# Attention outputs kept as features by tokens: row sums spread by transfers, the projection's operand in DRAM, VectorE and SyncE in source order

## The chip, the cores and the metric

The kernel runs on one core of one Trainium2 chip. The metric is the device time of one execution in microseconds (us). "Before" is the kernel as it was, "after" the kernel with the change below.

## The reference

The reference is one transformer block with adaptive layer norm, for 2048 tokens of 576 features, all in float32. The attention has 32 heads of 18 features; the gated feed-forward part has 4608 hidden features.

```
mod = (silu(c) @ w_mod).reshape(1, 6, 1, 576)      # sa, ca, ga, sb, cb, gb
h = layernorm(x) * (1 + ca) + sa
q, k, v = split(h @ wqkv)                          # 32 heads of 18
p = softmax(q @ k.T * 18 ** -0.5)                  # 2048 x 2048 for each head
x = x + ga * ((p @ v) @ wo)
h = layernorm(x) * (1 + cb) + sb
x = x + gb * ((sigmoid(h @ w_gate) * (h @ w_up)) @ w_down)
```

## The kernel before

Matrix products are taken in the fast float32 form, whose operands are rounded. To keep precision each operand is split into a rounded high part and a low part (the rest), and a product is the sum of three: high by high, high by low, low by high. A "copy to float32r" makes the high part, a subtraction the low part.

**Attention.** A unit is one pair of heads for one half (1024) of the queries; there are 32 units, first the 16 pairs for half 0, then for half 1. A unit has 16 steps (`kt`), one for each 128 keys. A step computes four transposed score tiles ("t", line 927: keys by queries, with the row maximum carried as two extra features of q), their exponentials on ScalarE (line 931), and four value products ("v", line 548), which collect in one PSUM bank. The values matrix has a column of ones, so that the sum of the exponentials comes out as feature 18 of each head. Beside that, a step does four of the 64 score tiles ("m", line 446) whose row maxima (line 452 on VectorE) the next unit needs. In most units two neighbouring maxima tiles are joined: ScalarE writes relu of the differences (line 455), and VectorE reduces once (line 457); that moves 8 of 64 operations a unit from VectorE to ScalarE. Units in `SINGLE` don't do that. PSUM tiles of "m", "t" and everything else are drawn by `bank()` from a ring of seven.

The order within a step is a string, one for even and one for odd `kt`. "k" stands for taking the finished sums out of PSUM (`taken`), "w" for work beside attention. There is one "w" in each two steps, so a unit is eight pairs of steps with one "w" each. At a "w" the kernel does, in this order, the outputs of the unit before (at `kt` 3), the spreading of the next unit's maxima (`spread`, line 485, four small transfers of `mrows` into the rows of q), and one piece of the generator `rows0` or `rows1`.

`load_heads(u + 2)` stands at the top of unit u. It issues eight transfers on SyncE's queue: for each head of the pair the high and low parts of q (36 and 18 rows of 4 KB) and of k (36 and 18 rows of 10 KB).

**Outputs.** `outputs()` transposes the finished 128x512 tile (32 rows for each head and query chunk, features by queries) in four TensorE transposes to tokens by features (line 572), takes the reciprocal of the sums on VectorE (line 576), copies the tile on ScalarE (line 587) and multiplies on GpSimd into `Oa` or `big` (line 591).

**Projection.** `project_o(t)` handles one tile of 128 tokens in pieces: transpose the outputs to features by tokens and split them (piece 1), the same for the last 64 features in the first half (piece 2), then two half-width products with `wo` of 14 matmuls each in the first half and 9 in the second (line 685, pieces 3 and 4). `rows0` does this for half 0, then the second layer norm and the operands of the gated stage; `rows1` projects half 1 as far as feature 384, and `last_rows` adds the remaining features during the gated stage, from `oend` in DRAM.

**Beside that** GpSimd splits w_down for the later stage in units 4 to 15 (`down_parts`, lines 841 to 848), with loads paced by the steps of attention.

**Order.** TensorE follows the source order in attention (a manual schedule). The order on the other engines and on SyncE's queue is written by a planner, which goes by its own estimate of times. Each engine, and each queue of transfers, works strictly in the order that it was given.

**Gated stage.** 18 blocks of 256 hidden features for each half of the tokens, with seven products for each block of a fast 2x2 scheme (line 1028) and the down projection (line 1064).

The lines of the strings:

```
for does in (("vtmmttmvtm", "tmttkwmtmm") if plain else ("vmmttmmtvt", "mtkttmwmmt"))[kt % 2]:
    ...
    elif does == "w":
        if kt == 3:
            outputs()
```

Of the kernel before, what the change touches and what calls it, by code (L numbers as in the profile page):

```python
# [15 lines left out]
F32 = mybir.dt.float32  # L16
# [24 lines left out]
FROM0, FROM1 = 15 * 16, 27 * 16 + 5  # L41
# [7 lines left out]
SINGLE = (0, 1, 16, 17, 18, 19, 20, 27, 28, 29)  # L49
# [6 lines left out]
def tile_block(ctx, tc, x_in, wqkv, wo, w_gate, w_up, w_down, c_in, w_mod, out):  # L56
# [24 lines left out]
    turns = {"s": 0, "to": 64 + 4 * LEAD, "bank": 0}  # L81
# [155 lines left out]
    oend = dram.tile([P, 8, D - DL], F32, name="oend")  # L237
# [288 lines left out]
    Os = [Oa]  # L526
# [10 lines left out]
    pending = []  # L537

# [18 lines left out]
    def taken():  # L557

        if "whole" in state:
            half, p, acc = state.pop("whole")  # L560
            oT = epool.tile([P, 512], F32, name="oT")
            nc.scalar.copy(oT, acc)
            state["end"] = (half, p, oT)

    def outputs():

        if "end" not in state:
            return
        half, p, oT = state.pop("end")
        tp = bank().rearrange("p (b q) -> p b q", q=P)  # L570
        for b in range(4):
            nc.tensor.transpose(tp[:, b, :], oT[:, b * P : (b + 1) * P], ident)  # L572

        tq = tp.rearrange("p b (j e) -> p j b e", e=32)
        rec = epool.tile([P, 4, 4], F32, name="rec")
        nc.vector.reciprocal(rec, tq[:, :, :, DH])
        if half == 1 and p == H // 2 - 1:
            state["last"] = epool.tile([P, 512], F32, name="oT")[:, 0 : 16 * DH].rearrange("p (t e) -> p t e", t=8)
            for h in range(2):
                nc.vector.tensor_tensor(  # L580
                    state["last"][:, :, h * DH : (h + 1) * DH].rearrange("p (c b) e -> p c b e", c=2),
                    tq[:, 2 * h : 2 * h + 2, :, 0:DH],
                    rec[:, 2 * h : 2 * h + 2, :].unsqueeze(3).to_broadcast([P, 2, 4, DH]),
                    op=ALU.mult,
                )
            return
        nc.scalar.copy(oT, tp.rearrange("p b q -> p (b q)"))
        tq = oT.rearrange("p (b j e) -> p j b e", j=4, e=32)
        for h in range(2):
            f0 = (2 * p + h) * DH  # L590
            nc.gpsimd.tensor_tensor(
                Os[half][:, :, f0 : f0 + DH].rearrange("p (c b) e -> p c b e", c=2),
                tq[:, 2 * h : 2 * h + 2, :, 0:DH],
                rec[:, 2 * h : 2 * h + 2, :].unsqueeze(3).to_broadcast([P, 2, 4, DH]),
                op=ALU.mult,
            )
# [6 lines left out]
    def load_wo():  # L603
# [31 lines left out]
        for _ in range(4):  # L635
            yield

    def project_o(t):

        wo_h, wo_l, we = weights  # L640
        T, T_ = temp([P, 2048], F32R), temp([P, 2048], F32)
        xt, full, od = T_[:, 0:D], T_[:, 1024:1536], T_[:, 1536:1664]
        if t >= 8:
            xt = raws.tile([P, 2, 3, 256], F32, name="raw1", bufs=2).rearrange("p v t c -> p (v t c)")[:, 0:D]
        nc.gpsimd.dma_start(xt, x_rows[:, t, :])
        src = Os[t // 8][:, t % 8, :]
        n = 4 if t < 8 else DL // P
        oh = T[:, 0 : n * P]
        ol = T[:, 512 : 512 + n * P]
        pt = bank()  # L650
        for i in range(n):
            nc.tensor.transpose(pt[:, i * P : (i + 1) * P], src[:, i * P : (i + 1) * P], ident)
        if t >= 12:
            nc.vector.tensor_copy(oh, pt[:, 0 : n * P])
            nc.vector.tensor_sub(ol, pt[:, 0 : n * P], oh.bitcast(F32))
        else:
            full = full[:, 0 : n * P]
            nc.vector.tensor_copy(full, pt[:, 0 : n * P])
            nc.gpsimd.tensor_copy(oh, full)
            nc.gpsimd.tensor_sub(ol, full, oh.bitcast(F32))  # L660
        yield
        if t < 8:
            om = T[:, 1024:1152]
            omh = T[:, 1152:1280]
            nc.gpsimd.tensor_copy(
                od.rearrange("p (a e) -> p a e", e=64), src[:, DM:D].unsqueeze(1).to_broadcast([P, 2, 64])
            )
            pt = bank()
            nc.tensor.transpose(pt[:, 0:P], od, ident)
            nc.vector.tensor_copy(od, pt[:, 0:P])  # L670
            nc.gpsimd.tensor_copy(om[0:64], od[0:64])
            nc.gpsimd.tensor_copy(omh[64:P], od[64:P])
            nc.gpsimd.tensor_sub(om[64:P], od[64:P], omh[64:P].bitcast(F32))
            yield
        for h in range(2):
            cols = slice(h * HALF, (h + 1) * HALF)
            ts_ = []
            for i in range(n):
                a, b = oh[:, i * P : (i + 1) * P], ol[:, i * P : (i + 1) * P]
                ts_ += [(a, wo_h[:, i, cols]), (a, wo_l[:, i, cols]), (b, wo_h[:, i, cols])]  # L680
            if t < 8:
                ts_ += [(om, we[:, 0, cols]), (om, we[:, 1, cols])]
# [6 lines left out]
        if t >= 8:  # L689
            nc.gpsimd.dma_start(x1p[:, t - 8, :], xt)  # L690
# [589 lines left out]
```

## Time and profile before

| | |
|---|---|
| median of 3 runs | 2932.13 us (2930.23 to 2935.79) |
| profiled execution | 2929.86 us, span 2927.5 us, granted clock 0.995 |
| attention, first to last score step | about 236 to 1594 us |
| gated stage | about 1599 us to the end |
| bytes moved | 429 MB, mean 147 GB/s |

Times in the profile count from the start of the span; the execution adds 2.4 us around it. "Busy" is the time in which an engine had an instruction running. An idle time is put down to the engine or transfer that released it. DMA share is the mean busy share of the core's 16 DMA engines.

### The profile page before, as it was taken

Reading aid. Unit: us, or ns where it says so; the run is one execution under the profiler, and the core shown is the slowest. Engines: PE = TensorE matmul, PEld = TensorE weight load, DVE = VectorE, ACT = ScalarE, POOL = GpSimd, SP = SyncE. Lnnn points to the kernel's source line nnn. Section 1 sums busy time; section 2 is a strip of 40 time slices with the busy share of each in tenths; the row PEclk is TensorE's granted clock in tenths of the full one; section 3 lists DMA queues with packets and bytes.
Section 4 is the critical chain, followed back from the end, with each engine's and each line's share of the span. In section 5 each row is a group of like instructions: output and inputs, shape, how many; then the busy total and the mean of one; then the engine's idle time right before and its main releaser. Section 6 shows DMA issues by size and latency. Waiting matters only on the chain.

```text
span 2927.5 us, 46356 instructions
## 1 busy us (share of the span) xinstructions
PE 2848.3 (97%) x17141; PEld 1879.6 (64%) x17141; DVE 2218.6 (76%) x4023; ACT 1581.4 (54%) x2955; POOL 649.4 (22%) x829
## 2 busy tenths in 40 slices
PE   7999999999999999999999899999999999999998
PEld 6964333333444444444443788877888888888888
DVE  7277888888899988999982878789777555555555
ACT  3216889999987778998788333333332111111111
POOL 3122014544213110761102222233221100000000
PEclk9999999999999999999999999999999999999999
DMA  5344124333212110222125866677556844554443
GB/s 180 120 157 128 52 76 140 133 120 123 84 56 76 35 56 23 101 98 66 52 87 177 284 216 234 231 277 247 207 201 233 301 170 167 167 168 167 159 159 136
DMA packets 136745, 429.25 MB, mean 147 GB/s; under 512 B 18884, under 2 KB 56520, under 8 KB 124232
## 3 DMA queue, kind: packets, MB, share of 16 engines
q1 hardware_dynamic: 120472, 344.99, 35.0%
q0 software_dynamic: 16048, 81.31, 7.9%
q8 instruction: 135, 2.21, 0.3%
q14 instruction: 90, 0.74, 0.1%
HBM read 267.77 MB, written 157.95 MB: 145 GB/s over the span
## 4 chain that ended last, share of the span: by engine, by line
PE 82%; DVE 7%; ACT 4%; DMA 3%; issue 3%; SPq 1%; POOL 0%; POOLq 0%; ACTq 0%; DVEq 0%
PE o L548 16%; PE d L1064 14%; PE x L1028 12%; PE s L446 11%; PE s L927 10%; PE bu L1028 4%; PE bg L1028 4%; PE s L274 4%; ACT p L931 3%; PE s L325 2%; PE s L685 2%; DVE mx L452 1%; DVE w L1020 1%; DMA B<-hs 1%; PE s L572 1%
## 5 line engine op out<-in xcount | busy, mean ns | idle before, releaser
L452 DVE TENSOR_REDUCE mx<-s 128x1 f32<-128x512 f32 x1696 | 1076.6, 684 | 126.3 <-PE s L446 108.3
L931 ACT ACTIVATE p<-s 128x512 f32<-128x512 f32 x2048 | 1068.4, 610 | 146.7 <-PE s L446 75.2
L446 PE MATMUL s<-k,q 54*128 54x512 f32 x1920 | 608.4, 451 | 12.2 <-ACT p L931 6.6
L548 PE MATMUL o<-p,vaug 128*32 128x512 f32 x4096 | 554.8, 607 | 0.5 <-ACT p L931 0.4
L927 PE MATMUL s<-q,k 56*128 56x512 f32 x1920 | 552.6, 425 | 1.3 <-DMA q<-mrows 0.8
L1064 PE MATMUL d<-wd,hh 128*128 128x288 f32 x2304 | 468.3, 297 | 20.8 <-DVE Oa L1068 20.2
L927 PEld LDWEIGHTS s<-q,k 56*128 56x128 f32 x1920 | 260.5, 186 | 295.2 <-DVE mx L452 184.7
L446 PEld LDWEIGHTS s<-k,q 54*128 54x128 f32 x1920 | 273.6, 184 | 250.3 <-ACT p L931 172.3
L1064 PEld LDWEIGHTS d<-wd,hh 128*128 128x128 f32 x2304 | 373.4, 188 | 35.6 <-DVE Oa L1068 26.4
L1068 DVE TENSOR_TENSOR Oa<-Oa,d 128x288 f32<-128x288 f32 x576 | 256.0, 452 | 125.5 <-PE d L1064 120.3
L1064 PE MATMUL d<-wd,hl 128*128 128x288 f32 x1152 | 340.7, 296 | 0.0
L1028 PE MATMUL x<-k,w 128*128 128x512 f32 x1008 | 242.4, 390 | 4.7 <-DVE u L1239 2.4
L1040 ACT ACTIVATE u<-u 128x512 f32<-128x512 f32 x72 | 45.5, 632 | 318.3 <-DVE u L1228 312.1
L1064 PEld LDWEIGHTS d<-wd,hl 128*128 128x128 f32 x1152 | 216.9, 188 | 0.0
L1028 PEld LDWEIGHTS x<-k,w 128*128 128x128 f32 x1008 | 186.7, 188 | 42.5 <-DVE u L1239 3.5
L548 PEld LDWEIGHTS o<-p,vaug 128*32 128x32 f32 x4096 | 83.4, 108 | 163.9 <-issue 151.4
L1037 ACT ACTIVATE sg<-x 128x512 f32<-128x512 f32 x36 | 21.5, 599 | 304.3 <-PE x L1028 304.3
L1070 POOL DMA_DIRECT2D out_dram<-Oa x16 | 8.7, 543 | 606.0 <-DVE Oa L1068 606.0
L455 ACT ACTIVATE over<-s 128x512 f32<-128x512 f32 x176 | 105.1, 597 | 33.5 <-PE s L446 28.4
L1028 PE MATMUL x<-big,w 128*128 128x512 f32 x504 | 120.6, 390 | 1.0 <-issue 1.0
L1028 PE MATMUL x<-w,w 128*128 128x512 f32 x504 | 121.0, 390 | 0.0
L457 DVE CUSTOM_DVE_ANT_0 over<-s,over 128x512 f32<-128x512 f32 x176 | 120.2, 683 | 0.3
(232 smaller groups left out, 3605.1 us busy)
## 6 DMA issues: line engine op xcount, KB each, us to landing
ws<-w SPq DMA_DIRECT2D x126, 640.0 KB
w<-ws SPq DMA_DIRECT2D x126, 640.0 KB
wd<-wds SPq DMA_DIRECT2D x36, 1152.0 KB
k<-kd SPq DMA_DIRECT2D x60, 360.0 KB
wds<-w POOLq DMA_DIRECT2D x18, 1152.0 KB, 4.5
k<-kd SPq DMA_DIRECT2D x60, 180.0 KB
w<-in_B_w_down_dram POOLq DMA_DIRECT2D x18, 576.0 KB, 4.3
q<-qd SPq DMA_DIRECT2D x64, 144.0 KB
```

The source lines that it names most:

```text
L274: nc.tensor.matmul(acc, w, hT[:, t, cols], start=n == 0, stop=n == len(ts_) - 1)
L325: nc.tensor.matmul(acc[:, 0:HALF], hT[:, k, rows], w, start=n == 0, stop=n == len(ts_) - 1,)
L446: nc.tensor.matmul(sp, qs[rows, qt * P : (qt + 1) * P], ks[rows, at * 512 : (at + 1) * 512], start=True, stop=True,)
L452: nc.vector.tensor_reduce(to, sp, axis=AX.X, op=ALU.max)
L455: nc.scalar.activation(over, sp, AF.Relu)
L457: nc.vector.tensor_tensor_reduce(out=over, in0=sp, in1=over, scale=1.0, scalar=LOWEST, op0=ALU.add, op1=ALU.max, accum_out=mx[:, h * n + q ...
L548: nc.tensor.matmul(acc[32 * j : 32 * j + 32, :], vaug[:, kt, (2 * p + h) * VW : (2 * p + h) * VW + 32], probs[2 * c + h], start=kt == 0, s ...
L927: nc.tensor.matmul(sT, ks[rows, kcols], qs[rows, c * 512 : (c + 1) * 512], start=True, stop=True)
L931: state["exp"] = nc.scalar.activation(pr, sT, AF.Exp, scale=SCALE)
L1028: nc.tensor.matmul(acc[v], w[:, v, a, :], X[s][:, b, :], start=first and n == 0, stop=n == 6, skip_group_check=not first,)
L1064: nc.tensor.matmul(acc[:, :HALF], a[:, f, rows], w[:, f, cols], start=n == 0, stop=n == 5)
L1068: nc.vector.tensor_add(Oa[:, t, cols], Oa[:, t, cols], acc[:, :HALF])
```

## The change

1. The outputs are no longer transposed. `outputs()` becomes four steps, one at each of the four "w" after the sums were taken (`kt` 1, 3, 5, 7 of the next unit). `gather` moves the four rows of sums by a transfer to 128 partitions. `spread` takes the reciprocal on VectorE, stores it to DRAM and loads it broadcast over each head's 32 rows. `scaled` multiplies on GpSimd, makes the high part and the low part. `stored` writes both, features by tokens, to `od` in DRAM with four transfers. All transfers are on SyncE's queue.
2. `project_o` loads its operands from `od`, one tile ahead, five transfers a tile on SyncE's queue (three in the second half), and has only the two product pieces. `last_rows` does the same instead of transposing.
3. VectorE's and SyncE's instructions in attention are put in source order, as TensorE's are.
4. Units 19 and 20 leave `SINGLE`, `rows1` starts four steps later, and `load_wo` has one more empty piece.

```diff
-FROM0, FROM1 = 15 * 16, 27 * 16 + 5
+FROM0, FROM1 = 15 * 16, 27 * 16 + 9
-SINGLE = (0, 1, 16, 17, 18, 19, 20, 27, 28, 29)
+SINGLE = (0, 1, 16, 17, 18, 27, 28, 29)
...
+    od = dram.tile([2, D, S], F32R, name="od")
+    rows_r = dram.tile([4, 512], F32, name="rows_r")
...
             oT = epool.tile([P, 512], F32, name="oT")
             nc.scalar.copy(oT, acc)
-            state["end"] = (half, p, oT)
+            todo_out.extend(outputs(half, p, oT))
...
+    def outputs(half, p, oT):
+        at = turns["out"] = (turns["out"] + 1) % 3
+        room = state["room"][:, 1536 * at : 1536 * (at + 1)]
+        full, parts = room[:, 0:512], room[:, 512:1536]
+        hi, lo = parts[:, 0:512], parts[:, 512:1024]
+        sums, rec = (epool.tile([P, 16], F32, name=n) for n in ("sums", "rec"))
+
+        def gather():
+            nc.sync.dma_start(sums, oT[DH::32, :].rearrange("j (q e) -> j q e", e=16))
+
+        def spread():
+            nc.vector.reciprocal(rec, sums)
+            nc.sync.dma_start(rows_r.rearrange("j (q e) -> (j q) e", e=16), rec)
+            nc.sync.dma_start(full, rows_r.unsqueeze(1).to_broadcast([4, 32, 512]))
+
+        def scaled():
+            nc.gpsimd.tensor_mul(full, full, oT)
+            nc.gpsimd.tensor_copy(hi.bitcast(F32R), full)
+            nc.gpsimd.tensor_sub(lo.bitcast(F32R), full, hi)
+
+        def stored():
+            for h in range(2):
+                f0 = (2 * p + h) * DH
+                for c in range(2):
+                    q, q0 = 32 * (2 * h + c), half * HW + c * 512
+                    nc.sync.dma_start(
+                        od[:, f0 : f0 + DH, q0 : q0 + 512].rearrange("l f q -> f l q").bitcast(F32),
+                        parts[q : q + DH].rearrange("f (l q) -> f l q", l=2),
+                    )
+        return [gather, spread, scaled, stored]
...
+    def load_o(t):
+        T = temp([P, 2048], F32R)
+        n = 4 if t < 8 else DL // P
+        cols = slice(t * P, (t + 1) * P)
+        for l in range(2):
+            nc.sync.dma_start(
+                T[:, 512 * l : 512 * l + n * P].rearrange("p (i q) -> p i q", q=P).bitcast(F32),
+                od[l, 0 : n * P, cols].rearrange("(i p) q -> p i q", p=P).bitcast(F32),
+            )
+            if t < 8:
+                nc.sync.dma_start(T[64 * l : 64 * l + 64, 1024:1152].bitcast(F32), od[l, DM:D, cols].bitcast(F32))
+        xt = Oa[:, t, :] if t < 8 else raws.tile(...)
+        nc.sync.dma_start(xt, x_rows[:, t, :])
+        return T, xt
...
-    manual.enter_context(tc.manual_schedule(engines={mybir.EngineType.PE}))
+    manual.enter_context(tc.manual_schedule(engines={mybir.EngineType.PE, mybir.EngineType.DVE, mybir.EngineType.SP}))
...
                 elif does == "w":
-                    if kt == 3:
-                        outputs()
+                    if todo_out:
+                        todo_out.pop(0)()
...
+    state["room"] = temp([P, 2048], F32)
+    turns["out"] = 2
     taken()
-    outputs()
+    for step in todo_out:
+        step()
     manual.close()
-    nc.sync.dma_start(oend[:, :, D - DL - 2 * DH :], state["last"])
```

140 lines of the change are left out of this document (34 added, 106 removed).

## The prediction

> **What bounds the kernel now.** I read the page first, then the groups of instructions inside two units of attention, then timelines of a few steps.
>
> ```profile
> span 2927.5 us, 46356 instructions
> PE 2848.3 (97%) x17141; PEld 1879.6 (64%) x17141; DVE 2218.6 (76%) x4023; ACT 1581.4 (54%) x2955; POOL 649.4 (22%) x829
> ```
>
> TensorE looks full, but its ends are modelled, so the page doesn't tell what sets the pace of a step. Attention is 32 units of 8 step pairs. Next come groups of unit 9 (no side work; 609.8 to 649.8) and of unit 17 (rows projected beside it; 937.2 to 985.9). Before the bar stand busy us and mean ns, behind it idle us and releaser.
>
> ```profile
> L931 ACT ACTIVATE p<-s 128x512 f32<-128x512 f32 x65 | 34.0, 611 | 0.9 <-PE s L927 0.4
> L452 DVE TENSOR_REDUCE mx<-s 128x1 f32<-128x512 f32 x48 | 30.9, 685 | 4.1 <-PE s L446 4.1
> ...
> L452 DVE TENSOR_REDUCE mx<-s 128x1 f32<-128x512 f32 x65 | 40.3, 680 | 0.1
> L931 ACT ACTIVATE p<-s 128x512 f32<-128x512 f32 x64 | 33.5, 603 | 14.2 <-PE s L927 7.4 <-PE s L446 6.8
> L685 PE MATMUL s<-w,t 128*128 128x288 f32 x48 | 7.4, 303 | 0.1
> ```
>
> In unit 9 ScalarE never waits (0.9 us of 40) and VectorE has 4.1 us to spare, 0.5 us a pair: a ScalarE-bound loop with VectorE close behind. In unit 17, where all maxima run on VectorE (SINGLE), VectorE is idle for 0.1 us; eight reduces of 40.3/65 = 0.62 us make 4.96 us a pair.
>
> The next fence has timeline rows (start us, us, engine): the values matmuls (L548) of two neighbouring plain pairs, then unit 8 around the outputs of unit 7.
>
> ```profile
> 505.91 1.06 PE L548 MATMUL o<-p,vaug 128*32 128x512 f32 x8
> 510.78 1.06 PE L548 MATMUL o<-p,vaug 128*32 128x512 f32 x8
> ...
> 571.96 0.62 ACT L562 COPY oT<-o 128x512 f32<-128x512 f32 x1
> 573.50 0.49 SPq L419 DMA_DIRECT2D k<-kd  x1
> 575.70 1.07 PE L548 MATMUL o<-p,vaug 128*32 128x512 f32 x8
> 577.60 0.66 PE L572 MATMUL s<-ident,oT 128*128 128x128 f32 x4
> 578.47 0.25 DVE L576 RECIPROCAL rec<-s 128x16 f32<-128x16 f32 x1
> 579.22 0.62 ACT L587 COPY oT<-s 128x512 f32<-128x512 f32 x1
> 580.98 1.06 PE L548 MATMUL o<-p,vaug 128*32 128x512 f32 x8
> ```
>
> A plain pair takes 510.78 - 505.91 = 4.87 us, the pair with the outputs 580.98 - 575.70 = 5.28: today's four transposes, reciprocal and second copy cost 0.41 us a unit, not their own 0.66 + 0.25 + 0.62.
>
> **The change part by part.**
>
> *Transposes and second copy out of outputs().* 31 units x 0.41 = 12.7 us less. The last unit is costed with the tail.
>
> *The projection of rows.* Its matmuls stay; the pairs that only transposed and split go. Here are one tile's four pairs in unit 18 (first half), then a transposing pair in the second half.
>
> ```profile
> 1011.25 1.06 PE L548 MATMUL o<-p,vaug 128*32 128x512 f32 x8
> 1016.62 1.07 PE L548 MATMUL o<-p,vaug 128*32 128x512 f32 x8
> 1023.10 1.07 PE L548 MATMUL o<-p,vaug 128*32 128x512 f32 x8
> 1029.96 1.06 PE L548 MATMUL o<-p,vaug 128*32 128x512 f32 x8
> 1035.56 0.64 PE L548 MATMUL o<-p,vaug 128*32 128x512 f32 x4
> ...
> 1425.60 1.07 PE L548 MATMUL o<-p,vaug 128*32 128x512 f32 x8
> 1430.83 1.06 PE L548 MATMUL o<-p,vaug 128*32 128x512 f32 x8
> ```
>
> The pairs are 5.37 (second transpose), 6.48 and 6.86 (matmuls), 5.60 (first transposes). Against 4.96 the two that go cost 0.41 + 0.64 = 1.05 us; 8 tiles give 8.4 us. In the second half 5.23 - 4.96 = 0.27, 8 tiles 2.2 us. The loads that replace them (five DMAs a tile, on SyncE) are asked two pairs, over 10 us, ahead of the matmuls; I cost them at nothing, and about 1 us a tile if they come late.
>
> *SINGLE without units 19 and 20.* 16 pairs go from 4.96 back to 4.87: 1.4 us. FROM1 four steps later moves work between units of the same kind: nothing.
>
> *The last rows.* 16 transposes leave the gated stage. Their two rows (ns: min/median/max):
>
> ```profile
> L1124 PE MATMUL d<-ident,od x8: 270/272/301, 1635.5 to 1705.4; 128*128 128x128 f32 x8
> L1131 PE MATMUL d<-ident,od x8: 272/272/273, 1636.4 to 1705.8; 128*128 128x128 f32 x8
> ```
>
> TensorE is the bound there, so 16 x 0.272 = 4.4 us.
>
> *VectorE and SyncE in source order.* VectorE's order in the timelines is the source's already wherever I followed it (maxima, reciprocal, mrows), so the order by itself costs nothing; bounds are -3 and +3 us for the modulate and layernorm pairs. What it does is fix where the new waits stand.
>
> *The new wait.* The gather of the sums is issued at the "w" of kt = 1. In source order eight transfers of load_heads stand ahead of it on SyncE; in unit 8 the last of them is issued at 573.50 + 0.49 = 573.99, so the gather leaves at about 574.0. The reciprocal waits for it at the "w" of kt = 3, where VectorE arrives at 578.47. So the gather has 4.5 us. Does it land in time? The windows below are unit 8, then unit 23 (two columns before the end of each row: DMA share of 16 engines, then GB/s).
>
> ```profile
> 576.50:578.50 2.00, 2.00 (x16) 1.17 (x13) 1.71 (x4) 1.90 (x5) 2.00 (x4) 1.00 0.60 196
> 578.50:580.50 2.00, 2.00 (x17) 0.83 (x16) 1.62 (x6) 1.92 (x5) 2.00 (x5) 1.00 0.59 153
> 580.50:582.50 2.00, 2.00 (x17) 0.75 (x15) 1.78 (x3) 1.99 (x4) 1.68 (x4) 1.00 0.27 103
> ...
> 1221.00:1223.00 2.00, 2.00 (x16) 1.23 (x13) 1.71 (x5) 1.90 (x5) 0.00 (x0) 1.00 0.59 179
> 1223.00:1225.00 2.00, 2.00 (x16) 0.83 (x15) 1.64 (x4) 1.92 (x5) 0.82 (x2) 1.00 0.09 26
> ...
> 1222.72 0.25 DVE L576 RECIPROCAL rec<-s 128x16 f32<-128x16 f32 x1
> ```
>
> The heads' data are still moving when the reciprocal's turn has come. The share stands near 0.59 and falls to 0.27, so in unit 8 the movement ends about 0.27/0.59 x 2 = 0.9 us into the last window, at 581.4; in unit 23 at 1223.3. The share says that 9 of the 16 engines work (9/16 = 0.56). [...]
>
> That a later transfer waits for earlier ones of its queue is seen in the gated stage:
>
> ```profile
> 1627.82 0.55 SPq L865 DMA_DIRECT2D raw<-in_B_w_up_dram  x1
> 1628.49 0.41 SPq L1119 DMA_DIRECT2D od<-oend  x1
> 1635.51 0.63 PE L1124 MATMUL d<-ident,od 128*128 128x128 f32 x4 [1.66 <-DMA od<-oend]
> ...
> wds<-w POOLq DMA_DIRECT2D x18, 1152.0 KB, 4.5
> ```
>
> TensorE waited for these 384 KB until 7.0 us after their issue behind loads of raw, while 1152 KB on GpSimd's queue land in 4.5 us (median). So I take the gather to land with the last head data, plus its own completion. For that the nearest row is a wait for a 1 KB transfer:
>
> ```profile
> SPq L146 <- DMA gates<-w: 4.3, 2, 3.4
> ```
>
> 4.3 us in 2 waits: 0.9 and 3.4, of which part may overlap the loads' end; I take 0.9. Then VectorE stalls 581.4 + 0.9 - 578.47 = 3.8 us in unit 8 and 1223.3 + 0.9 - 1222.72 = 1.5 us in unit 23. Bounds: nothing (if the small packets overtake) and 581.4 + 3.4 - 578.47 = 6.3.
>
> Queued behind the reciprocal on VectorE are the reduces that free the banks. The first bank behind it is drawn where the transposes stood, at 577.60, and asked for again seven draws later: a pair has 16 draws in 4.87 us, so 2.1 us on, at 579.7. Without a stall VectorE frees it at 578.47 + 0.25 + 0.69 (a reduce) = 579.4. So 0.3 us is absorbed and the rest reaches TensorE, and through it ScalarE, the bound.
>
> Units: 1 to 15 run beside the w_down transfers, as unit 8 does. Unit 8 gives 3.8 - 0.3 = 3.5; how much of that traffic meets the head loads differs from unit to unit, so I take 3.0: 15 x 3.0 = 45. Units 16 and 19 to 27 resemble unit 23: 10 x 1.4 = 14 (I round its 1.2 up, since load_o's transfers now go ahead of some loads). In 17, 18, 28 and 29 the pairs are 6.5 us, VectorE arrives 2 to 3 us later, and I take 0.5 each: 2. Units 30, 31 load no heads: 0. Sum 61 us; bounds 0 and 110.
>
> *GpSimd and SyncE behind it.* Reciprocal, two more DRAM transfers (the second broadcast), three 128x512 operations on GpSimd and four stores follow in a chain. SyncE must be free again for mrows at kt = 11; 10 us remain, so this costs nothing. Without that cover see the third rival.
>
> *The tail.* The last outputs wait for a gather instead of transposes while VectorE has the first weights to prepare: +1.5 us (0 to +6).
>
> **Sum.** 61 + 1.5 - 12.7 - 8.4 - 2.2 - 1.4 - 4.4 = +33.4 us. The profiled execution took 2929.9 (span 2927.5 and 2.4 around it), so 2963.3; the median of the runs shown, 2932.1, lies 2.3 above it, which gives **2965 us**. A measurement of this kernel can tell about 0.2%, 6 us, from no change.
>
> **The rivals.**
>
> *The gather overtakes or is quick.* Then only the savings count: 2932.1 + 1.5 - 29.1 = 2904 us. For it: the gather is 8 KB, 7 of the 16 engines are idle meanwhile, and 4.5 us is long. Against it: the late od above, on the same queue. It decides from the point where the gather lands before 578.8 (578.47 + 0.3). [...] Chance 0.23.
>
> *Half hidden.* [...] Chance 0.05.
>
> *The chain holds SyncE.* GpSimd works in order and waits for the paced w_down load and its landing:
>
> ```profile
> 588.33 0.77 POOL L826 DMA_DIRECT2D w<-in_B_w_down_dram  x1 [5.80 <-ACT p L931]
> 592.40 1.55 POOL L841 TENSOR_TENSOR w<-w,gb_b 128x288 f32<-128x288 f32 x2 [3.31 <-DMA w<-in_B_w_down_dram]
> ...
> 604.24 2.79 SPq L485 DMA_DIRECT2D q<-mrows  x4
> ```
>
> If the scaling is queued behind such a load (5.8 + 3.3 us) and one group of splits (3.9), the stores block SyncE past kt = 11, mrows come 3 us late for the next unit's first scores, and 12 units add 36 us: 3001. Chance 0.06.
>
> **How the numbers follow.** My forecast has 0.66, its own range 2940 to 2992. The range given reaches down to 2903, so that it takes in half of the quick gather, and leaves out its faster half (0.11) and the held SyncE. Faster 0.24 (the quick gather and a little of half hidden), same 0.04, slower 0.72.
>
> **What would show it.** L576 (the reciprocal) with idle time in front, released by a DMA into sums, some 2 to 4 us in 25 units; pair 1 of a plain unit at 7 to 8.5 us where it is 5.28; the other pairs still 4.87; ScalarE's exps gaining idle behind TensorE. Wrong if reciprocals start without a wait, if pair 1 is 4.9, or if the loss sits at the first scores of a unit behind mrows or load_o.

## The result: 5.3% slower, and the profile after

The changed kernel takes **3086.0 us** (median of 4 runs, 3078.8 to 3095.2), the kernel before 2931.2 beside it: a ratio of **1.0527 (1.0489 to 1.0565)**. The prediction was 2965 us, 2903 to 2992. Its sign and the place of its wait were right; what a stop of TensorE costs was not in it, and its size was a fifth of what came: +33 forecast, +155 measured. The profiled execution after took 3092.5 us, its span 3090.6.

The page, first lines:

```profile
span 3090.6 us, 46347 instructions
PE 2920.0 (94%) x16933; PEld 1888.2 (61%) x16933; DVE 2201.8 (71%) x3983; ACT 1577.6 (51%) x2940; POOL 686.6 (22%) x791
```

TensorE has 208 instructions fewer than before and is busy 72 us *longer*: each takes more time. Where the 163.1 us of span came in is told by the last score step: 1732.6 against 1591.7. So **140.9 us came in attention, 22.2 us behind it**.

The timeline of unit 8 after, beside the one that the prediction showed of before (last transfer of the heads, the copy, the gather, the values matmuls, the reciprocal):

```profile
614.02 0.62 ACT L563 COPY oT<-o 128x512 f32<-128x512 f32 x1
615.52 0.48 SPq L420 DMA_DIRECT2D k<-kd  x1
615.63 1.07 PE L549 MATMUL o<-p,vaug 128*32 128x512 f32 x8
616.11 0.61 SPq L578 DMA_DIRECT2D sums<-oT  x1
620.49 1.07 PE L549 MATMUL o<-p,vaug 128*32 128x512 f32 x8
624.55 0.25 DVE L581 RECIPROCAL rec<-sums 128x16 f32<-128x16 f32 x1 [3.95 <-DMA sums<-oT]
624.83 0.36 SPq L582 DMA_DIRECT2D rows_r<-rec  x1
625.41 1.10 PE L447 MATMUL s<-k,q 54*128 54x512 f32 x2 [3.18 <-DVE mx L458]
627.84 0.56 SPq L583 DMA_DIRECT2D Oa<-rows_r  x1
630.22 1.93 PE L549 MATMUL o<-p,vaug 128*32 128x512 f32 x8
```

The gather leaves right behind the heads, and its data are there 8.4 us later (616.11 to 624.55). VectorE has stood 3.95 us by then (3.8 forecast), TensorE 3.18. The pair that lost its transposes takes 620.49 - 615.63 = 4.86 us where it took 5.28, so that saving is real. The next takes 630.22 - 620.49 = 9.73: some 4.9 us more, for a wait of 3.95. The windows of these microseconds say why (TensorE's busy us first; third column from the end the granted clock):

```profile
622.00:624.00 2.00, 0.23 (x2) 0.00 (x0) 0.00 (x0) 1.09 (x2) 1.41 (x3) 1.00 0.13 29
624.00:626.00 2.00, 0.49 (x1) 0.18 (x1) 1.45 (x5) 0.60 (x1) 0.00 (x0) 1.00 0.89 369
626.00:628.00 2.00, 1.98 (x12) 0.55 (x14) 1.75 (x3) 0.60 (x1) 0.00 (x0) 0.76 0.59 225
628.00:630.00 2.00, 2.00 (x9) 1.31 (x9) 1.15 (x2) 1.32 (x3) 0.00 (x0) 0.50 0.11 23
630.00:632.00 2.00, 2.00 (x10) 0.20 (x8) 1.45 (x4) 1.24 (x3) 0.00 (x0) 0.50 0.26 100
632.00:634.00 2.00, 2.00 (x11) 1.16 (x7) 0.92 (x2) 1.05 (x3) 0.80 (x1) 0.54 0.03 12
```

After TensorE has stood, **its granted clock falls to half** for 6.8 us; with the clock at 0.50 it does 9 to 11 instructions in 2 us, at 1.00 it did 16. Over attention, before and after:

```profile
236.00:1592.00 1356.00, 1338.67 (x8802) 566.66 (x8802) 1172.77 (x2162) 1175.58 (x2317) 391.95 (x574) 0.99 0.26 85
236.00:1733.00 1497.00, 1403.39 (x8615) 569.95 (x8616) 1153.60 (x2134) 1174.28 (x2302) 423.40 (x533) 0.94 0.30 94
```

A mean of 0.94 over 1497 us is 0.06/0.5 of it, about 180 us, at half clock. Summed from the trace's clock records it is 13.7 us before and 177.5 after, nearly all in blocks of 3.41, 6.83 or 10.24 us.

The waits of attention after, then the last of them before (engine, line, waited for: us in all, times, longest):

```profile
DVE rec L581 <- DMA sums<-oT: 98.9, 29, 9.1
PE s L447 <- DVE mx L458: 51.5, 18, 4.3
DVE mrows L482 <- ACT mrows L481: 34.7, 31, 8.0
...
DVE mrows L481 <- ACT mrows L480: 17.3, 22, 8.0
```

The reciprocal waited 98.9 us, 9 of them in the last unit where nothing hangs on it; 90 us fall in units 1 to 29. And VectorE now waits twice as long for ScalarE's half of the mean rows: the new source order at work (experiment 3).

The tail after, then the first product of before:

```profile
1736.98 0.56 SPq L578 DMA_DIRECT2D sums<-oT  x1
1739.34 0.25 DVE L581 RECIPROCAL rec<-sums 128x16 f32<-128x16 f32 x1 [33.12 <-DMA sums<-oT]
1746.91 1.26 POOL L586 TENSOR_TENSOR t<-t,oT 128x512 f32<-128x512 f32 x1 [13.10 <-DMA t<-rows_r]
1750.70 1.57 SPq L595 DMA_DIRECT2D od<-t  x4
1758.64 0.83 ACT L1010 CAST w<-raw 128x768 fp32r<-128x768 f32 x1 [21.68 <-DMA od<-t]
1759.52 1.22 PE L1019 MATMUL x<-k,w 128*128 128x512 f32 x2
...
1599.17 3.44 PE L1028 MATMUL x<-k,w 128*128 128x512 f32 x14 [2.35 <-ACT w L1019]
```

The first product of the gated stage comes 26.9 us after attention instead of 7.5. Everything waits for the stores of the last outputs: ScalarE's weight tile by 21.68 us.

### The profile page after: what moved, and what is told of

It reads as the page before. It is cut to its first block, busy times and chain, and to the rows that moved or that the text cites. A ratio compares the mean times of both kernels' runs of the same rounds, so it can differ in the third digit from the quotient of the medians.

```text
span 3090.6 us, 46347 instructions
## 1 busy us (share of the span) xinstructions
PE 2920.0 (94%) x16933; PEld 1888.2 (61%) x16933; DVE 2201.8 (71%) x3983; ACT 1577.6 (51%) x2940; POOL 686.6 (22%) x791
## 3 DMA queue, kind: packets, MB, share of 16 engines
q1 hardware_dynamic: 154424, 375.67, 36.7%
## 5 line engine op out<-in xcount | busy, mean ns | idle before, releaser
L453 DVE TENSOR_REDUCE mx<-s 128x1 f32<-128x512 f32 x1664 | 1056.5, 684 | 175.3 <-PE s L447 155.4
L447 PE MATMUL s<-k,q 54*128 54x512 f32 x1920 | 655.3, 473 | 73.1 <-DVE mx L458 51.5
L918 PE MATMUL s<-q,k 56*128 56x512 f32 x1920 | 583.4, 447 | 12.4 <-DVE mx L453 6.1
L549 PE MATMUL o<-p,vaug 128*32 128x512 f32 x4096 | 586.4, 639 | 0.5 <-ACT p L922 0.4
L447 PEld LDWEIGHTS s<-k,q 54*128 54x128 f32 x1920 | 294.4, 193 | 373.9 <-ACT p L922 218.0
L1055 PE MATMUL d<-wd,hh 128*128 128x288 f32 x2304 | 471.6, 299 | 20.7 <-DVE Oa L1059 20.5
L918 PEld LDWEIGHTS s<-q,k 56*128 56x128 f32 x1920 | 271.9, 196 | 312.7 <-DVE mx L453 223.9
L456 ACT ACTIVATE over<-s 128x512 f32<-128x512 f32 x192 | 114.6, 597 | 90.4 <-DVE mx L458 38.5
L458 DVE CUSTOM_DVE_ANT_0 over<-s,over 128x512 f32<-128x512 f32 x192 | 129.8, 676 | 0.6
```

Source lines behind the costliest of these rows:

```text
L447: nc.tensor.matmul(sp, qs[rows, qt * P : (qt + 1) * P], ks[rows, at * 512 : (at + 1) * 512], start=True, stop=True,)
L453: nc.vector.tensor_reduce(to, sp, axis=AX.X, op=ALU.max)
L456: nc.scalar.activation(over, sp, AF.Relu)
L458: nc.vector.tensor_tensor_reduce(out=over, in0=sp, in1=over, scale=1.0, scalar=LOWEST, op0=ALU.add, op1=ALU.max, accum_out=mx[:, h * n + q ...
L549: nc.tensor.matmul(acc[32 * j : 32 * j + 32, :], vaug[:, kt, (2 * p + h) * VW : (2 * p + h) * VW + 32], probs[2 * c + h], start=kt == 0, s ...
L918: nc.tensor.matmul(sT, ks[rows, kcols], qs[rows, c * 512 : (c + 1) * 512], start=True, stop=True)
```

## The experiments

**How the numbers below were taken.** "Attention" is the time of the last score step in the profiled execution, "rest" the span from there on, "half clock" the time at the halved clock within attention, from the trace's clock records. Each ratio goes by the kernel before on the same chip (medians 2931.2 to 2933.8). In the short diffs `PE`, `DVE`, `SP` stand for the names of the engines, and "..." for what is left as it is.

| kernel | median us | ratio to before (95%) | attention | rest | half clock |
|---|---|---|---|---|---|
| before | 2931.2 | 1 | 1591.7 | 1335.8 | 13.7 |
| after | 3086.0 | 1.0527 (1.0489, 1.0565) | 1732.6 | 1358.0 | 177.5 |
| 1 reciprocal one pair later | 2973.2 | 1.0146 (1.0123, 1.0170) | 1616.7 | 1355.6 | 37.6 |
| 2 heads behind the gather | 3031.3 | 1.0332 (1.0307, 1.0356) | 1669.5 | 1358.7 | 92.1 |
| 3 before, order written out | 2947.0 | 1.0053 (1.0034, 1.0072) | 1609.8 | 1337.0 | 17.1 |
| 4 idle transposes in the wait | 3069.4 | 1.0466 (1.0432, 1.0500) | 1694.8 | 1359.6 | 51.2 |
| 5 gather on GpSimd's queue | 3097.7 | 1.0562 (1.0544, 1.0579) | 1738.0 | 1362.1 | 167.3 |
| 6 TensorE's order alone | 2997.4 | 1.0228 (1.0211, 1.0245) | 1636.4 | 1358.0 | 71.7 |
| 7 room for the last outputs | 3070.0 | 1.0479 (1.0453, 1.0506) | 1721.5 | 1343.8 | 150.2 |
| 8 = 1 + 6 + 7 | 2986.0 | 1.0179 (1.0164, 1.0194) | 1635.8 | 1341.8 | 75.1 |
| 9 = 6 + 7, stores on GpSimd | 2967.8 | 1.0114 (1.0097, 1.0131) | 1618.0 | 1352.1 | 54.6 |
| 10 = 9, load with more lead | 2959.9 | 1.0090 (1.0075, 1.0105) | 1610.3 | 1349.0 | 54.6 |
| 11 no gather | 3071.5 | 1.0482 (1.0463, 1.0501) | 1708.9 | 1357.4 | 133.1 |
| 12 = 10, loads on GpSimd | 2949.1 | 1.0066 (1.0047, 1.0086) | 1594.0 | 1352.5 | 41.0 |
| 13 = 12 + 11 | 3046.8 | 1.0394 (1.0370, 1.0420) | 1697.7 | 1347.4 | 160.4 |
| 14 = 12, tail's two transfers on GpSimd | 2945.9 | 1.0049 (1.0035, 1.0062) | 1585.3 | 1353.3 | 13.7 |

**1. The reciprocal one pair later.**

```
-        return [gather, spread, scaled, stored]
+        return [gather, lambda: None, spread, scaled, stored]
```

> The reciprocal (with the two transfers behind it) comes one "w", about 4.9 us of attention, later; nothing else is changed. Theory A (VectorE waits for the gather, which lands behind the heads' transfers; the halted TensorE then also gets half its clock): the 90 us of waits before the reciprocal in units 1 to 29 fall below 10, time at half clock in attention from 178 to under 40 us, pair 2 of a plain unit from 10 to 12 us back to about 4.9, and the kernel to about 2940 us. Theory B (the source order of VectorE and SyncE or the new loads of the projection are what costs): the waits go, but the kernel stays above 3040 us.

Measured: 2973 us. The stalls are gone but for a few (3.9 us in unit 3, 14.1 in the last unit):

```profile
DVE rec L581 <- DMA sums<-oT: 24.0, 9, 14.1
```

With 80 us of stalls (of the 90 in units 1 to 29) and 140 us of half clock, 116 us of attention go. So the wait in front of the reciprocal, with the clock behind it, is most of the loss. That it stays 33 us above A's 2940 left something to find.

**2. The heads' transfers behind the gather.**

```
-        if 0 < u < UNITS - 2:
-            load_heads(u + 2)
...
+                    if kt == 1 and 0 < u < UNITS - 2:
+                        load_heads(u + 2)
```

(the second place is the "w", right behind the gather.)

> The heads' eight transfers are issued right behind the gather in SyncE's order, not ahead of it. If the gather is late because it stands in a queue behind them (A), it lands some 2 to 3 us after its issue, before VectorE asks for it: waits before the reciprocal under 10 us in all, the kernel at about 2940 us, as with the later reciprocal. If the gather itself is slow (128 pieces of 64 bytes out of four rows), it still takes 8 us, and the kernel stays near 3086 us.

Measured: 3031 us. With the heads behind it on SyncE's queue the gather is never late: VectorE waits nowhere in front of the reciprocal in units 1 to 30. That shows what made it late: the heads' transfers ahead of it. Whether it waits for its turn in their queue or for something that it shares with them on any queue, this experiment doesn't tell (experiment 5 does). But TensorE now stands at the beginnings of units, for the mean rows:

```profile
597.67 0.58 SPq L583 DMA_DIRECT2D Oa<-rows_r  x1
613.18 0.59 POOL L840 DMA_DIRECT2D wds<-w  x1 [0.30 <-POOL w L835]
613.79 1.29 POOL L586 TENSOR_TENSOR Oa<-Oa,oT 128x512 f32<-128x512 f32 x1
615.20 0.28 DVE L482 TENSOR_TENSOR mrows<-s,mrows 16x128 fp32r<-16x128 f32 x1 [0.93 <-ACT mrows L481]
617.14 1.41 SPq L595 DMA_DIRECT2D od<-Oa  x4
618.65 2.77 SPq L486 DMA_DIRECT2D q<-mrows  x4
624.36 0.60 PE L918 MATMUL s<-q,k 56*128 56x512 f32 x2 [2.83 <-DMA q<-mrows]
```

The mean rows are made at 615.48. Their transfer is issued at 618.65, because the stores of the outputs stand ahead of it on SyncE, which waits there for GpSimd's scaling; and GpSimd does that behind its share of w_down. This is the prediction's third rival, "the chain holds SyncE", in its mechanism: 36.7 us in 9 waits, where it had 36 in 12 units. In the changed kernel itself it doesn't come up: TensorE's waits for the mean rows there are one of 0.3 us.

**3. The order alone.** In the kernel before:

```
-    manual.enter_context(tc.manual_schedule(engines={PE}))
+    manual.enter_context(tc.manual_schedule(engines={PE, DVE, SP}))
```

> The kernel before, with VectorE and SyncE in source order in attention and nothing else. If the order costs by itself (it puts the subtraction for mrows ahead of a reduce that could run meanwhile; in the changed kernel pair 7 is 5.46 us where it was 4.86), the kernel takes 15 to 20 us more, about 2948 us, and pair 7 shows 5.4 to 5.5 us. If the order is free, as the prediction had it, 2931 us.

Measured: 2947 us, attention +18.1. The waits of VectorE there:

```profile
DVE mrows L481 <- ACT mrows L480: 34.7, 31, 8.0
```

It is the row of the changed kernel, to the tenth; with the planner's order it was 17.3 us in 22 waits. In source order the subtraction of the mean rows stands one reduce too early, and VectorE waits for ScalarE where the planner had let it work. The last pair of a plain unit takes 5.46 us instead of 4.86.

**4. TensorE kept busy in the wait.**

```
+                        if kt == 3 and u < UNITS - 2:
+                            fill = bank()
+                            for _ in range(16):
+                                nc.tensor.transpose(fill[:, 0:P], ident, ident)
```

> The changed kernel with 16 idle transposes (2.6 us of TensorE) behind the reciprocal's place in each unit, so that TensorE works through most of VectorE's wait. If the halved clock after the halt is a cost of its own (about 0.38 us lost for each us at half clock), time at half clock in attention falls from 178 to under 60 us and the kernel to about 3040 us although TensorE has 80 us more to do. If the halved clock is harmless beside the waits, the kernel gets no faster, 3085 to 3110 us.

Measured: 3069 us, between the two forecasts: the time at half clock falls as far as the first had it, from 177.5 to 51.2, and the kernel gets only 17 us faster by the medians (attention 37.8 us shorter in the profiled executions). The stalls stay (94.8 us against 98.9, the last unit in both). Work for nothing makes the kernel faster: the clock is a cost of its own beside the wait. Its price can be read from units that differ in it. From the starts of the score matmuls, pair 2 with its stall takes 7.25 us in unit 25 (stall 2.50, no half clock), 9.10 in unit 14 (3.17, 3.41 us at half clock) and, with pair 3, 17.43 in unit 12 (4.23, 10.24): beyond the stalls (9.10 - 7.25 - 0.67)/3.41 and (17.43 - 12.11 - 1.73)/10.24, 0.35 us for each us at half clock. The whole is then about 164 x 0.35 = 57 us. This is an estimate; the filler took away 126 us of half clock and returned 38.

**5. The gather on GpSimd's queue.**

```
-            nc.sync.dma_start(sums, oT[DH::32, :]...)
+            nc.gpsimd.dma_start(sums, oT[DH::32, :]...)
```

> The changed kernel with one edit: the gather of the sums is issued on GpSimd's queue in place of SyncE's; the reciprocal keeps its place. Theory A: the gather lands late because it stands behind the heads' eight transfers in SyncE's queue. On the other queue it lands about 2 us after its issue, the stalls before the reciprocal in units 2 to 16 fall under 0.5 us each, the halved clock goes with them, and the time is that of the kernel with the late reciprocal: 2960 to 2990 us. Rival B: the sixteen DMA engines are shared, and the gather's packets wait behind the heads' packets whichever queue issued them: it still lands 7 to 9 us after its issue and the time stays at 3070 to 3095 us.

Measured: 3098 us, B's number, and for two reasons. In units 5 to 12 the gather is issued late. Unit 8:

```profile
621.04 0.62 ACT L563 COPY oT<-o 128x512 f32<-128x512 f32 x1
629.68 0.58 POOL L840 DMA_DIRECT2D wds<-w  x1 [0.30 <-POOL w L835]
630.25 0.72 POOL L578 DMA_DIRECT2D sums<-oT  x1
634.61 0.25 DVE L581 RECIPROCAL rec<-sums 128x16 f32<-128x16 f32 x1 [6.98 <-DMA sums<-oT]
```

The sums are ready at 621.66 and the gather is issued at 630.25, behind GpSimd's share of w_down. From there it takes 4.4 us. One queue of waiting was exchanged for another. In units 1 to 4, 13 to 19 and 24 to 29 it is issued within 1.6 us of the copy, while the heads' transfers, issued on SyncE's queue, are under way. There it lands 6.1 to 10.3 us after its issue (in units 13 to 15 7.5 to 8.0, with 2.1 to 2.5 us of stall), and that is B's reason. The last three gathers, with no loads of heads beside them, land in 2.1 to 2.2 us. From unit 5 to the end:

```profile
DMA to landing us min/median/max: 2.1/5.8/8.0
```

So the heads' data hold up a gather on another queue too: its place in SyncE's queue is not the whole cause.

**6. The written order for TensorE alone.** The edit of experiment 3 reversed, in the changed kernel.

> The changed kernel with one edit: the order written out by hand holds for TensorE alone, as before the change; VectorE and SyncE are ordered by the planner. Theory A: the source order costs what it cost by itself in the kernel before (14.7 us, the last pair of a unit 5.46 us against 4.86), and the reciprocal stays where it is: 3060 to 3075 us, with the stalls before the reciprocal in place. Rival B: the source order is what holds the reciprocal ahead of the reduces; the planner puts it behind them, the stalls fall under 1 us and the clock stays up: 2940 to 2970 us.

Measured: 2997 us, between both. B's mechanism is right: the planner puts reduces ahead of the reciprocal, and no stall in front of it is left in attention up to unit 29. Plain units take 39.6 us, 0.4 less than before. But TensorE waits for other things:

```profile
PE s L918 <- DMA q<-mrows: 36.0, 9, 10.1
PE s L679 <- DMA t<-od: 18.4, 2, 9.5
```

The chain of experiment 2 again, and the first load of the projection in units 16 and 27.

**7. Room for the last outputs.** `full`, `hi` and `lo` of the last unit are three tiles of the probabilities' pool:

```
-    state["room"] = temp([P, 2048], F32)
+    state["room"] = None        # outputs() then takes ppool tiles p0, p1, p2
```

> The changed kernel with one edit: the outputs of the last unit are scaled and split in three tiles of the pool that holds the probabilities, and not in a temporary of the pool whose space the first weight tiles of the gated stage take next. Theory A: the 27 us between the end of attention and the first product of the gated stage are the wait of these weight tiles for the outputs' stores; without it they come back to 8 to 10 us and the time falls by 15 to 20 us, to 3066 to 3071 us; attention stays at 1733 us. Rival B: the probabilities' space too is taken again at once, or the reciprocal's own wait on VectorE holds the stage's first operations: less than 5 us, 3081 to 3090 us.

Measured: the rest 1343.8 us, 14.2 less; the first product comes 5.2 us after attention, sooner than before (7.5). So the 27 us were the wait of the first weight tiles for space that the last outputs still used. (Attention is 11 us shorter in this execution with the same code: 27 us less at half clock.)

**8. Three repairs together** (1, 6 and 7).

> The changed kernel with three edits at once: the reciprocal one step later, the last unit's outputs in the probabilities' pool, and the written order for TensorE alone. Theory A (three costs that add): 2973 of the late reciprocal alone, less about 15 for the order and about 19 for the tail: 2935 to 2945 us, the kernel before within 0.5%; what is left over it is the wait for the first load of the projection (5.5 us) and for the mean rows. Rival B (the costs cover one another): one of the two edits buys nothing beside the late reciprocal, 2952 to 2975 us. Rival C: the savings that the change was worth show once the waits are gone: 2900 to 2920 us.

Measured: 2986 us, none of the three. The two repairs of the reciprocal are the same repair twice, and with the planner's order SyncE's chain costs more than with the written one: attention ends at 1635.8, 19 us later than in experiment 1. The waits of SyncE:

```profile
SPq L605 <- POOL Oa L592: 161.6, 15, 21.4
SPq L605 <- POOL big L592: 111.7, 14, 10.7
```

SyncE stands 273 us in front of the stores, waiting for GpSimd.

**9. The stores on GpSimd's queue,** behind the operations that make their data (with 6 and 7).

```
         def stored():
...
-                    nc.sync.dma_start(od[...], parts[...])
+                    nc.gpsimd.dma_start(od[...], parts[...])
```

> The changed kernel with the written order for TensorE alone, the last unit's outputs in the probabilities' pool, and the outputs' four stores issued on GpSimd's queue, behind the three operations on GpSimd that make their data. With the planner's order the stalls before the reciprocal are gone, but TensorE waits 36 us in 9 places for the mean rows' transfers, which stand on SyncE's queue behind the outputs' stores, and SyncE waits there for GpSimd (273 us in 29 places). Theory A (the waiting store holds the mean rows back): the nine gaps go, with the clock that they cost, and the time is 2940 to 2955 us; the two waits for the first load of the projection, 19 us with their clock about 27, stay. Rival B (the mean rows are late by the broadcast, which stands ahead of them too and waits for the reciprocal's transfer, or by their own producer): the gaps stay and the time is 2970 to 2990 us.

**10. More lead for the projection's first load.**

```
         ahead = load_o(t0)
         yield
+        yield
```

> The kernel with the stores on GpSimd's queue and one edit more: the first load of each half's projection gets one more step (two key tiles) of lead before the products that read it. Theory A (the products of unit 16 and unit 27 wait 9 to 10 us each for a load that was issued too late): both waits go, with their clock 20 to 27 us less than the kernel with the stores alone: 2913 to 2935 us, faster than the kernel before or level with it. Rival B (the load is late because it waits for the store of the last unit of the half, which cannot be earlier): one of the two waits stays, 2930 to 2950 us; or the step pushes the rows' work into the end of attention and costs what it gains.

Measured: 2968 and 2960 us, 13 and 25 us slower than the upper ends of their A; 9 lies just under the range of its B, 10 is 10 us over its own. In 9 TensorE waits for the mean rows 15.1 us in 4 places, against 36.0 in 9 in kernel 6: the stores were one cause, and not the only one. In 10 it waits for the projection's load 10.2 us instead of 19.6. What is left, at the end of unit 15 of kernel 10:

```profile
898.80 1.27 POOL L590 TENSOR_TENSOR Oa<-Oa,oT 128x512 f32<-128x512 f32 x1
902.38 2.45 POOL L605 DMA_DIRECT2D od<-Oa  x4 [0.29 <-POOL Oa L592]
904.78 0.93 SPq L658 DMA_DIRECT2D t<-od  x2
905.81 2.79 SPq L486 DMA_DIRECT2D q<-mrows  x4
```

The planner has put a load that reads `od` ahead of the mean rows on SyncE, and that load waits for the stores, which wait behind `wo` on GpSimd. TensorE stands 11.5 us.

**11. No gather.** One transfer spreads the rows from a reciprocal of the whole tile:

```
         def gather():
-            nc.sync.dma_start(sums, ...)
+            nc.vector.reciprocal(full, oT)
         def spread():
-            nc.vector.reciprocal(rec, sums)
-            ... two transfers through DRAM
+            nc.sync.dma_start(hi, full[DH::32, :].unsqueeze(1).to_broadcast([4, 32, 512]))
```

> The changed kernel with one edit: no gather of the sums. VectorE takes the reciprocal of the whole 128x512 copy where the gather stood, and one transfer spreads the four rows of sums from it, so VectorE waits for no transfer; the order stays written out for three engines. Theory A (the wait for the gather's transfer is the cost, 90 us, and the halved clock behind it about 62): both go and the time is that of the late reciprocal or somewhat less, 2945 to 2975 us; VectorE has some 0.5 to 1 us more a unit to do, 15 to 30 us if it bounds the unit. Rival B (the reciprocal of 128x512 takes several us and stalls TensorE as the wait did): over 3020 us. In the tail two transfers fewer: 5 to 8 us less from attention to the first product.

Measured: 3072 us, Rival B. The reciprocal in the kernel (ns: min/median/max):

```profile
L576 DVE RECIPROCAL big<-oT x16: 3342/3343/3353, 959.5 to 1679.7; 128x512 f32<-128x512 f32 x16
```

3.34 us for 512 elements a row, 0.25 for 16. VectorE waits for no transfer here, works for these 3.3 us, and the loss is nearly that of the changed kernel. The 5 to 8 us that the tail was to gain did not come (first product 27.5 us after attention, 26.9 in the changed kernel). So the loss doesn't hang on the transfer as such: with VectorE kept from its reduces by 3.34 us of work, as by the wait of 3.95 us in unit 8 of the changed kernel, TensorE stops (41.9 us in 20 waits for the maxima), and 133.1 us of attention are at half clock (177.5 in the changed kernel). By the two reciprocals an element takes (3.343 - 0.253)/496 = 6.2 ns, where a reduce of 512 has 0.684/512 = 1.3.

**12. The projection's loads on GpSimd's queue** (all of `load_o`, with 10).

> The kernel with the written order for TensorE alone, the stores on GpSimd's queue and the load with more lead, and one edit more: the projection's loads of its operand and its rows of x are issued on GpSimd's queue. Theory A (the load waits on SyncE's queue for the store of the unit before, and the mean rows stand behind it: 11.5 us in unit 15): that gap and most of the other waits for the mean rows go: 2935 to 2950 us. Rival B (on GpSimd's queue the loads come behind its own work and the products of the projection wait instead): 2960 to 2975 us.

Measured: 2949 us, A. Unit 15 takes 40.9 us instead of 52.5, TensorE's waits for the mean rows sum to 0.5 us, and attention ends at 1594.0, 2.3 us from where it ended before.

**13. 12 with the edit of 11.**

> The kernel with the loads on GpSimd's queue and the edit of e11: no gather, one spreading transfer from the whole reciprocal. Theory A (the rest is waits of the chain, attention's and the tail's): 5 to 12 us less than the kernel with the loads alone, 2925 to 2942 us, level with the kernel before. Rival B (VectorE's longer reciprocal costs what the shorter chain brings): level with the kernel with the loads alone or up to 20 us slower.

Measured: 3047 us, far over its B: the long reciprocal stops TensorE in nearly every unit, now in pieces of 1.4 us and less in most units. It shows after how little the clock can halve (unit 4, 1.65 us of idle time within 4; windows as above):

```profile
424.00:426.00 2.00, 0.96 (x7) 0.29 (x3) 2.00 (x2) 1.31 (x3) 0.00 (x0) 1.00 0.68 175
426.00:428.00 2.00, 1.39 (x4) 0.55 (x4) 2.00 (x5) 1.01 (x2) 0.00 (x0) 1.00 1.03 221
428.00:430.00 2.00, 2.00 (x12) 0.32 (x10) 1.34 (x3) 0.67 (x2) 0.00 (x0) 0.50 0.66 153
```

In units 1 to 15 such a stop (1.5 to 1.8 us) was followed by half clock 13 times. In units 7 and 12 it was not, and their pair 1 takes 7.5 us, against 8.7 in units 4, 6, 8 and 11 with the same stop and 3.41 us at half clock. That is (8.71 - 7.51)/3.41 = 0.35 us for each us at half clock, the price of experiment 4 again, from one and the same stop.

**14. The tail's two transfers of the reciprocals on GpSimd's queue,** with 12, and one `yield` more as in 10.

> The kernel with the loads on GpSimd's queue and two edits: in the last unit alone the reciprocals' two transfers are issued on GpSimd's queue (on SyncE's the second waits 6.5 us for the first to land, and the weight loads of the gated stage stand behind it, 8 us later than in the kernel before), and the projection's first load has one more step of lead. Theory A (these two places are the rest): 8 us of the tail and 5 to 12 us of the two loads and their clock go: 2929 to 2938 us, level with the kernel before (2931.6). Rival B (GpSimd itself is late: it waits in the tail for the same transfer, and its sums for the weight tiles come after): the tail keeps its 17 us and the time stays at 2940 to 2950 us.

Measured: 2946 us. In attention there is nothing left of the loss: in the profiled execution (2940.4 us) it ends at 1585.3, **6.4 us earlier than before**, with the half clock of before. The loss, 17.5 us, lies behind it: Rival B. GpSimd in the tail:

```profile
1601.22 0.74 POOL L588 DMA_DIRECT2D p<-rows_r  x1 [4.46 <-DMA rows_r<-rec]
1611.23 1.31 POOL L591 TENSOR_TENSOR p<-p,oT 128x512 f32<-128x512 f32 x1 [9.27 <-DMA p<-rows_r]
```

It stands 13.7 us for two transfers while the weight sums of the gated stage are its next work, and by the 112th product matmul the stage is 14.0 us behind where the kernel before was. The other kernels with room for the last outputs point the same way. With the stores on SyncE (7 and 8) the stage is 0.3 and 1.1 us behind at that product; with the stores on GpSimd (9, 10 and 12), which issues them for 4.1 us ahead of these sums, it is 9.7, 8.4 and 9.0. But kernel 7 has attention's losses, and its rest ends 8.0 us longer than before all the same, lost later in the stage. Both repairs in one kernel were not tried. No version beats the kernel before.

## Why the prediction was wrong in size and right in sign

**The wait and its place: right.** The gather lands behind the heads (experiment 2 shows it; the reason given, their order in one queue, is too narrow, since experiment 5 has it as late on another), VectorE waits in front of the reciprocal, and the reduces queued behind it stop TensorE. Unit 8 stalls 3.95 us where 3.8 were worked out. The rival "overtakes or is quick" did not happen, nor did "half hidden": the stalls are 3.7 us a unit in units 1 to 15 and 3.2 in 16 and 19 to 27. A gather landed 2.1 to 2.2 us after its issue with nothing beside it (experiment 5); in unit 8 of the changed kernel it took 8.4.

**"Units 16 and 19 to 27 resemble unit 23: 10 x 1.4": mis-sized.** Their stalls sum to 31.7 us instead of 14, 3.2 a unit; unit 23 itself has 3.2 instead of 1.2. Units 1 to 15 have 56.0 in all, 3.7 each, or 3.4 net of the 0.3 absorbed, against 3.0. All stalls net of that are about 81 us against 61.

**"0.3 us is absorbed and the rest reaches TensorE": the step that failed.** The rest reaches TensorE and then costs once more, since the clock halves behind it. The sum took a stall as its own length. Experiments 1 and 4 show that it isn't: about 57 us by the 0.35 us estimated above, which kernel 13 gives a second time. The page before had the clock in each window row, at 1.00; nothing in it showed a halved clock behind a wait, and the prediction didn't ask what TensorE's stop does to it. The runs show it: in the changed kernel's attention the half clock comes in blocks of 3.41, 6.83 or 10.24 us, and in experiment 13 it came after 1.65 us of idle time within 4 (the last section has the count over all traces).

**"The order by itself costs nothing; bounds are -3 and +3": wrong.** It costs 14.2 us by the medians (2947.0 against 2932.9 on the same chip), 18.1 in attention. I had followed VectorE's order in the timelines and found the source's; the one place that differs, the subtraction of the mean rows one reduce earlier, passed unseen. The row that answers is in the waits, 17.3 against 34.7 us.

**"The tail: +1.5 (0 to +6)": wrong.** It is +19.4 (26.9 - 7.5). I costed the wait for the gather, and not that the last outputs lie in a temporary whose space the gated stage takes next, so that their whole chain with its four transfers stood in front of the first weight tile. Experiment 7 took back 14.2 us.

**The savings.** The 0.41 us a unit is there (4.86 against 5.28). Of the 8.4 us of the projected rows nothing arrives: units 16 to 21 take 290.3 us in experiment 1 against 287.0 in experiment 3, in part because the first product waits for its load (pair 5 of unit 16 takes 12.0 us instead of 6.5); what took the rest was not settled. I had costed the loads at nothing, or 1 us a tile if late. Of the last rows' 4.4 us nothing is seen either: behind the tail the rest is 2.8 us longer (22.2 - 19.4). The stage is 16.1 us behind before at the 112th product and 24.0 at the 672nd. Into this stretch fall four blocks of half clock, 20.5 us, where before has one of 3.4; what set them off was not settled.

**"The chain costs nothing":** right for the changed kernel, wrong for its nearest relatives (experiments 2, 6, 8), where it costs 33 to 37 us of waits and the clock behind them.

Together, in attention: stalls 81 + clock 57 + order 18 - outputs 12 = 144, of 140.9 measured; the tail 19.4 and 2.8 behind it make 163.1. The terms overlap, so the agreement is no proof of each. The three that experiments took away by themselves (the wait with its clock, the order, the tail) are shown; the clock's share alone is an estimate, with its price read twice.

## What to carry to other kernels

Where a wait stops TensorE for 1.5 us or more in a stage that it else fills, count the wait and then the halved clock that came behind it here in most cases (13 of 15 stops of 1.5 to 1.8 us in kernel 13), an estimated 0.35 us for each of the next 3.4 to 10 us. When a small transfer is to feed a compute engine, ask what is ahead of it on its queue, what else is being moved while it waits, and what is behind the waiting instruction on the engine, and put a step between issue and use; here one pair was worth 113 us. And of every step that waits on a shared queue (a store for its producer, a load for a store) ask which urgent transfer stands behind it: moving it to its producer's own queue repaired attention (1636.4 us in kernel 6, 1594.0 in kernel 12), and holding the same queue up for 13.7 us in the tail spent it again (kernel 14).

## What the runs showed of the hardware that was not expected

- The granted clock halved after TensorE had been idle for 1.65 us within 4 (kernel 13, unit 4). In the attention of the changed kernel it stayed at half for 3.41, 6.83 or 10.24 us. Not every stop had this behind it: in unit 25 of the changed kernel a stop of 1.75 us (stall 2.50) was followed by none.
- Where a stop fell went with it. In each execution all half-clock blocks start on one grid of 3.413 us, at another phase in each. Over the attention of all 16 traces (from 330 us on), a window of this grid at full clock was followed by half clock in all 129 cases in which TensorE was idle for 1.6 us of it or more, in none of 5566 with less than 0.6, and in 50 of 161 between; of these, the kernel before and the changed kernel have 21 of 21, none of 692 and 5 of 14. The grid cuts the stop of unit 25 into 1.11 and 0.79 us, and that of kernel 13's unit 7 into 1.24 and 0.62; unit 4 there has 1.64 in one window. (The idle time is read from matmul records, whose ends are modelled.)
- Sixteen 128x128 transposes in the gap, whose results nobody reads, were enough to bring the half clock of attention from 177.5 to 51.2 us.
- An 8 KB gather landed 2.1 to 2.2 us after its issue with nothing beside it, and 6.1 to 10.3 us after it beside loads of 72 to 360 KB issued on another queue (experiment 5).
- A reciprocal on VectorE takes 0.25 us for 128x16 and 3.34 for 128x512.
- A transfer that reads what the one before it wrote to DRAM could be issued 3.0 us after that one in unit 8 (624.83 to 627.84), but 6.1 us after it in kernel 14's tail with other traffic (1595.15 to 1601.22; GpSimd waits 4.46 of them).
